# A table of gates laid out by expert, through a small scratch in DRAM, in an attention and two-layer mixture-of-experts kernel

## The chip, the cores and the metric

The kernel runs on one core of one Trainium2 chip. The metric is the device time of one execution in microseconds (us). Of the kernel before three executions were timed; their median is 2020.06 us.

## The reference

Attention over 4 batches, 8 heads, 576 positions and 64 values per head (local in heads 0 to 3, strided in heads 4 to 7) gives a matrix x of N = 2304 tokens by 512. The first layer mixes eight experts densely, with weights P from a Sinkhorn iteration. The second layer sends each token to exactly one expert, each expert with room for 288 tokens, in the order of the logits.

```python
def _moe_ref(x, w_gate, w1, w2):          # first layer: x (2304, 512), 8 experts, 1024 hidden
    logits = x @ w_gate
    P = np.exp(logits - logits.max())
    for _ in range(8):
        P /= P.sum(1, keepdims=True) + 1e-09
        P /= P.sum(0, keepdims=True) + 1e-09
        P *= N / E
    for e in range(E):
        out += P[:, e:e + 1] * (np.maximum(x @ w1[e], 0.0) @ w2[e])

def _moe2_ref(x, w_gate, w1, w2):         # second layer, on the output of the first
    logits = x @ w_gate                   # w_gate (512, 8)
    order = np.argsort(-logits.flatten())
    ...                                   # each token to the first expert in this order that has room
    for e in range(E):
        out[assigned == e] = np.maximum(x[assigned == e] @ w1[e], 0.0) @ w2[e]
```

## The kernel before

The work is one long program for five engines, written out in Python loops.

**Start.** Attention (`attention`, 0 to about 300 us) is cut into pieces. The string `SEQ` is the hand-written order in which its pieces (A), the preparation of the first expert's weights (W, V; R loads the second matrix), the first pieces of the next batch (E) and the first products of the first expert (Q) are issued. In this part every engine takes its instructions in the order in which they are written. That holds for the queue on which SyncE issues DMAs too (SPq in the profile); an issue that must wait holds up all issues behind it. Ahead of the loop over `SEQ` stand the load of the first expert's first matrix (L1443, 2 MB), that of the first layer's gates (L653) and that of the second layer's gates into the tile `wg2` (L1445). `wg2` (128 partitions x 4 x 8 floats) is not read by anything in the kernel before. The E pieces follow: `att_early` loads v of the next batch head by head (`att_load_v`, L176 to L179), waits `EPAD` = 3 pieces, and takes the largest absolute values on VectorE (`att_scale`, L207 and L210).

**First layer.** For each expert and each block of 512 tokens (256 for the first expert), `l1` makes 8 banks of 12 products (L729), and each bank is emptied by ScalarE into `hh` (L732) and by VectorE into `hl` (L733). There are three such banks, so TensorE waits when L733 is late. `l2` makes 24 products for a tile of 128 tokens (L747), and VectorE adds the result to `acc` (L779). `blocks` alternates the first product of one block with the second product of the block before. `weave` mixes other pieces in between in a fixed proportion, and `behind` queues each piece behind the last emptying of a bank.

**Logits of the second layer.** They are needed for routing, and are formed on VectorE in float32. `logits` (L904) multiplies a tile of `acc` (128 x 512) by the gates of one expert, which `gate_bcast` has copied into every partition, and sums along the row. Eight instructions make a tile's logits. The tiles named in `LATE` (8 to 15) get theirs woven into the last but one block order, before the last expert's share is added (1417 to 1506 us); for them `late_w` has multiplied the last expert's second matrix by the gates (L929, two halves of 256 columns, 128 instructions, 820 to 946 us), and `late_logits` adds that share by small products (L954, L955). The other ten tiles get their logits at once behind their last `l2` (1556 to 1694 us), next to `x2_rows` (L871 to L888), which scales and stores the tokens' rows.

`gate_bcast` loads rows d0 to d0 + n of the gates, 512 x 8 floats in memory, into each partition as they lie: the eight experts' gates of one row are next to each other, so the gates of one expert, `g[:, :, e]`, are read in steps of 8 floats.

**Second layer.** `routing` closes one expert after another, in pieces between the products that are left, and `ffn` computes the experts (to the end).

Of the kernel before, what the change touches and what calls it, by code (L numbers as in the profile page):

```python
# [33 lines left out]
# the order of the pieces of attention (A), both matrices of the first expert (W, V; R loads the second), what comes  # L34
# early of the second batch (E), products of the first expert (Q) and the gates (G, H)
# [29 lines left out]
class Arena:  # L65
    """Tiles as parts of others that are no longer needed."""
# [25 lines left out]
class Kernel:  # L92
# [11 lines left out]
    def abank(self, b, name):  # L104
        """While there is no first layer yet, attention has its banks too."""
        return self.bank(name, "l1" if b == 0 and name in ("ps", "po") else "bank")
# [5 lines left out]
    def pow2_scale(self, pool, top, mx, name):  # L112
        """From |max| in every partition: the power of two that takes it into [top/2, top), and its inverse."""
        nc = self.nc
        s = pool.tile([128, 1], F32, name=name)
        i = pool.tile([128, 1], F32, name=name + "_i")
        nc.vector.tensor_scalar(i, mx, 2.0 / top, 1e-30, op0=OP.mult, op1=OP.max)
        nc.vector.tensor_scalar(i.bitcast(I32), i.bitcast(I32), 0x7F800000, None, op0=OP.bitwise_and)
        nc.vector.reciprocal(s, i)  # L119
        return s, i  # L120

    # ---------------------------------------------------------------- attention
    def att_consts(self, pool):
# [3 lines left out]
        # local: query q and key window position k (key = q0 - 32 + k): 1 <= k - q <= 32  # L127
# [9 lines left out]
        # strided: position 4 i + r; the same r, and no later i  # L137
# [18 lines left out]
    def busy(self, ps, n):  # L156
        """Products that nothing needs, in front of those of a bank: the clock of the array follows its load."""
# [4 lines left out]
    def att_load_v(self, b, parts=None):  # L162
        """v of a batch: of every kind and head a part with room for a last column."""
# [35 lines left out]
    def att_scale(self, b):  # L199
        """The scale of a batch, from its values."""  # L200
# [17 lines left out]
        # token c * 128 + p belongs to batch token // 576  # L218
# [11 lines left out]
    def att_v(self, b, kind):  # L230
        """v in two halves, the high one with a column of ones, in 4 pieces."""
# [28 lines left out]
    def att_qk(self, u):  # L260
        """q and k of a pair of heads, transposed and in two halves."""
# [29 lines left out]
    def att_s(self, u, j):  # L291
        """Scores of one head, masked."""
# [27 lines left out]
    def att_e(self, u, j, i):  # L320
        """The exponentials of the scores of one head, first or second half."""
# [5 lines left out]
    def att_s_exact(self, u, j, kq, sm):  # L327
        """The same by products in float32, with the masks added and the sums taken on the way."""
# [56 lines left out]
    def over(self, x, ov, name):  # L385
        """Values over the sums of their weights."""
# [7 lines left out]
    def att_o(self, u, j):  # L394
        """The exponentials of one head, transposed."""
# [23 lines left out]
    def att_o2(self, u, j):  # L419
        """The values of one head, by the exponentials, over their sums."""  # L420
# [37 lines left out]
    def attention(self):  # L458
        """Attention, in pieces; after the last one of a batch its number is yielded."""
# [77 lines left out]
    def att_side(self, b):  # L537
        """What a batch does next to its heads: the second half of its v, and the first of that of the next one."""
# [10 lines left out]
    def att_early(self, pool):  # L549
        """What of the second batch comes before its heads, in 18 + EPAD pieces."""  # L550
# [10 lines left out]
    # ---------------------------------------------------------------- weights  # L561
# [8 lines left out]
    def loading(self):  # L570
        """Pieces without work, for as long as a matrix comes in."""
# [10 lines left out]
    def w_scale(self, r, j, inv, early):  # L582
        """The scale of a matrix of an expert; inv: the inverses of both of its matrices, multiplied."""
# [43 lines left out]
    def w_prep(self, e, w, raw=None, js=(0, 1)):  # L627
        """The weights of an expert of the first layer in two halves, in 8 pieces each."""
# [21 lines left out]
    # ---------------------------------------------------------------- gates of the first layer  # L650
# [19 lines left out]
    def gate(self, c0, c1):  # L670
        """Logits of tiles c0 to c1."""
# [15 lines left out]
    def sinkhorn(self):  # L687
# [7 lines left out]
        # the eighth power of the exponential of an eighth: the table is closest near 0  # L695
# [22 lines left out]
    # ---------------------------------------------------------------- the first layer  # L718
    def l1(self, w, t0, nb, h):
        """h = relu(x w1), transposed and in two halves."""  # L720
# [16 lines left out]
    def l2(self, w, t0, nb, h, done, fine=False):  # L737
        """y = h w2 of a tile of tokens, handed to done."""
# [44 lines left out]
    def pairs(self, jobs, pool, nb):  # L783
        """jobs as those of blocks: the first products of two, then the second ones, in small pieces."""
# [8 lines left out]
    def blocks(self, jobs, pool, nb, fine=False):  # L793
        """jobs: (expert, weights, first token, tokens); the first product of one runs before the second of the one before."""
# [11 lines left out]
    def weave(self, *gens):  # L806
        """(generator, its weight): all of them, evenly; a piece yields its weight, or weighs 1."""
# [9 lines left out]
    def behind(self, gen):  # L817
        """Every piece is queued behind what empties the last bank of a product traced before it."""
# [8 lines left out]
    def traced(self):  # L827
        """The last instructions so far of the engines that the pieces run on."""
# [15 lines left out]
    # ---------------------------------------------------------------- between the layers  # L844
    def m2_prep(self, e):
        """The weights of an expert of the second layer, in two halves, to DRAM, in 16 pieces."""
# [19 lines left out]
    def x2_rows(self, c):  # L866
        """A tile of tokens of the second layer, scaled by token and in two halves, to DRAM."""
# [32 lines left out]
    def logits(self, c):  # L900
        """Of a tile of tokens, of what is summed so far."""
        for e in range(E):
            junk = self.m2.tile([128, DM], F32, name="junk")
            self.nc.vector.scalar_tensor_tensor(junk, self.acc[:, c], 1.0, self.wgb[:, :, e], op0=OP.mult,  # L904
# [4 lines left out]
    def gate_bcast(self, o, d0, n):  # L909
        """The gates of the second layer in every partition, rows d0 on."""  # L910
        g = self.a["moe2_w_gate"]
        self.nc.sync.dma_start(out=o, in_=bass.AP(tensor=g.tensor, offset=g.offset + d0 * E, ap=[[0, 128], [1, n * E]]))
        return o.rearrange("p (d e) -> p d e", e=E)

    def late_w(self):
        """The second matrix of the last expert, times the gates of the second layer, in two halves, in 65 pieces."""
# [3 lines left out]
        for i in range(2):  # L920
# [5 lines left out]
            for c in range(FC):  # L926
                for e in range(E):
                    junk = self.m2.tile([128, DM], F32, name="junk")
                    nc.vector.scalar_tensor_tensor(junk[:, :n], w[:, c], 1.0, g[:, :, e], op0=OP.mult, op1=OP.mult,  # L929
# [14 lines left out]
    def late_logits(self, t0, nb, h):  # L944
        """What the last expert adds to the logits of a block, from its first product."""
# [17 lines left out]
    # ---------------------------------------------------------------- the second layer: who goes where  # L963
    def route_consts(self):
# [30 lines left out]
        # the state: who is free, room (far from any count once closed), closed experts, the assignment  # L995
# [8 lines left out]
        # rows that the first list takes another way  # L1004
# [7 lines left out]
    def search(self, key, oh, remc, base, first):  # L1012
        """The largest threshold, from base on, where an expert has as many keys as room."""
# [24 lines left out]
    def route(self, ph):  # L1038
        """Close one expert: every token that goes somewhere before it is full is assigned."""
# [13 lines left out]
        # the order of floats as that of two 16-bit numbers; 0 for tokens that have their place  # L1053
# [17 lines left out]
        # counts at the threshold and above it  # L1071
# [12 lines left out]
        # of every expert: the tokens above, and those at the threshold  # L1084
# [7 lines left out]
        # the first expert that is full, in ones, and its rows of weights  # L1092
# [471 lines left out]
```

## Time and profile before

| | |
|---|---|
| median of three runs | 2020.06 us (2018.05 to 2022.18) |
| profiled execution, first to last instruction | 2046.9 us |
| mean granted clock of TensorE in it | 0.974 |
| TensorE busy | 1944.9 us, 95% |
| VectorE busy | 1253.3 us, 61% |
| L904 on VectorE | 144 instructions, 156.2 us |
| L929 on VectorE | 128 instructions, 79.6 us |

The profiled execution is one execution, and no time but its span is known for it: the span is its own time here, 1.3% above the median of the runs. An engine is busy while one of its instructions runs; TensorE's matmuls overlap, so the mean of one is longer than the distance to the next. A wait names the instruction that waited and what released it. The granted clock is a share of full speed.

### The profile page before, as it was taken

What the parts mean: (1) busy time and instruction counts of PE and PEld (TensorE: products, weight loads), DVE (VectorE), ACT (ScalarE), POOL (GpSimd) and SP (SyncE); (2) the same over time, 40 slices, a digit from 0 to 9 for tenths busy, and PEclk for the clock granted to TensorE, in tenths of its full rate; (3) what the DMA queues carried; (4) which work ended last, traced back from release to release, by engine and by line L of the source; (5) the groups of instructions that cost most, each with busy time, mean ns of one, the idle gap of its engine ahead of it and who ended that gap; (6) DMA issues with size and microseconds to landing.
All of it is one profiled execution on the core that took longest, in us unless ns stands there. A gap on an engine that the chain in (4) does not pass through costs nothing.

```text
span 2046.9 us, 30815 instructions
## 1 busy us (share of the span) xinstructions
PE 1944.9 (95%) x12796; PEld 1102.4 (54%) x12796; DVE 1253.3 (61%) x2934; ACT 542.8 (27%) x1053; POOL 192.4 (9%) x272
## 2 busy tenths in 40 slices
PE   8899999999999999999999999999899889998997
PEld 7768676444544544454445444545354334676676
DVE  7777668365545545875555465435956898765530
ACT  5555553132222222111221222212101100122232
POOL 1433300000000000000000000000000002222231
PEclk9789999999999999999999999999999999999999
DMA  8212102024313431111243234401000002335350
GB/s 206 61 36 63 24 30 96 1 83 164 117 50 134 162 114 42 42 42 42 83 146 110 74 113 154 144 29 54 0 1 11 21 21 98 133 117 189 118 212 24
DMA packets 106300, 172.04 MB, mean 84 GB/s; under 512 B 61456, under 2 KB 64016, under 8 KB 101680
## 3 DMA queue, kind: packets, MB, share of 16 engines
q1 hardware_dynamic: 98480, 127.07, 18.8%
q0 software_dynamic: 7680, 43.01, 5.9%
q8 instruction: 100, 1.64, 0.3%
q14 instruction: 40, 0.33, 0.0%
HBM read 126.53 MB, written 43.53 MB: 83 GB/s over the span
## 4 chain that ended last, share of the span: by engine, by line
PE 60%; DVE 25%; DMA 7%; issue 4%; ACT 2%; POOL 1%; another core or an unknown queue 1%; SPq 0%; POOLq 0%; DVEq 0%; ACTq 0%
PE l L729 23%; PE l L747 23%; DVE junk L904 6%; DMA raw<-in_moe_w_dram 5%; PE mm L1384 3%; DVE junk L929 3%; DVE wmx L588 3%; PE mm L1356 2%; DVE hl L733 2%; DVE acc L779 1%; DVE m2l L616 1%; DVE w2l L616 1%; PE pcnt L1025 1%; DVE w1l L616 1%
## 5 line engine op out<-in xcount | busy, mean ns | idle before, releaser
L729 PE MATMUL l<-xh,w1h 128*128 128x512 f16 (+1 forms) x1408 | 484.5, 344 | 41.9 <-DVE hl L733 41.3
L729 PE MATMUL l<-xl,w1h 128*128 128x512 f16 (+1 forms) x1408 | 484.3, 344 | 0.0
L729 PE MATMUL l<-xh,w1l 128*128 128x512 f16 (+1 forms) x1408 | 484.1, 344 | 0.0
L747 PE MATMUL l<-w2h,hh 128*128 128x512 f16 x1152 | 438.1, 380 | 0.0
L747 PE MATMUL l<-w2l,hh 128*128 128x512 f16 x1152 | 437.8, 380 | 0.0
L747 PE MATMUL l<-w2h,hl 128*128 128x512 f16 x1152 | 437.5, 380 | 0.0
L729 PEld LDWEIGHTS <-w1h 128*128 128x128 f16 x2816 | 276.1, 99 | 276.5 <-issue 54.9
L732 ACT ACTIVATE hh<-l 128x512 f16<-128x512 f32 (+1 forms) x352 | 180.7, 517 | 805.9 <-PE l L729 805.7
L747 PEld LDWEIGHTS <-hh 128*128 128x128 f16 x2304 | 222.3, 98 | 258.7 <-issue 3.3
L733 DVE SCALAR_TENSOR_TENSOR hl<-l,hh 128x512 f16<-128x512 f32 (+1 forms) x352 | 205.6, 591 | 221.4 <-ACT hh L732 221.4
L779 DVE SCALAR_TENSOR_TENSOR acc<-l,pe,acc 128x512 f32<-128x512 f32 x126 | 94.2, 748 | 176.2 <-PE l L747 176.2
L729 PEld LDWEIGHTS <-w1l 128*128 128x128 f16 x1408 | 139.2, 99 | 114.4 <-issue 3.0
L747 PEld LDWEIGHTS <-hl 128*128 128x128 f16 x1152 | 113.0, 98 | 136.6 <-issue 1.3
L588 DVE TENSOR_REDUCE wmx<-raw 128x1 f32<-128x1024 f32 x120 | 141.2, 1210 | 65.6 <-DMA raw<-in_moe_w_dram 65.5
L904 DVE SCALAR_TENSOR_TENSOR junk<-acc,raw 128x512 f32<-128x512 f32 x144 | 156.2, 1084 | 3.3 <-DMA raw<-in_moe_w_gate_dram 1.4
L612 ACT ACTIVATE m2h<-raw,wscale 128x1024 f16<-128x1024 f32 x64 | 70.4, 1141 | 187.8 <-DVE iw L601 85.2
L616 DVE SCALAR_TENSOR_TENSOR m2l<-raw,wscale,m2h 128x1024 f16<-128x1024 f32 x64 | 80.1, 1281 | 45.6 <-DMA wd<-m2l 28.2
L594 POOL PARTITION_ALL_REDUCE wall<-wmx x32 | 11.3, 352 | 974.2 <-DVE wmx L592 974.2
L929 DVE SCALAR_TENSOR_TENSOR junk<-raw 128x256 f32<-128x256 f32 x128 | 79.6, 622 | 12.5 <-DMA raw<-in_moe_w_dram 9.0
L1361 DVE SCALAR_TENSOR_TENSOR h2l<-mm,h2h 128x288 f16<-128x288 f32 x64 | 28.8, 452 | 61.6 <-ACT h2h L1360 53.8
L612 ACT ACTIVATE w2h<-raw,wscale 128x1024 f16<-128x1024 f32 x28 | 30.1, 1137 | 94.9 <-DVE wscale L119 94.9
L1360 ACT ACTIVATE h2h<-mm 128x288 f16<-128x288 f32 x64 | 25.2, 411 | 91.8 <-PE mm L1356 66.5
(379 smaller groups left out, 2173.9 us busy)
## 6 DMA issues: line engine op xcount, KB each, us to landing
raw<-in_moe_w_dram SPq DMA_DIRECT2D x30, 2048.0 KB
wd<-m2h SPq DMA_DIRECT2D x32, 512.0 KB
wd<-m2l SPq DMA_DIRECT2D x32, 512.0 KB
q<-in_q_dram SPq DMA_DIRECT2D x32, 144.0 KB
k<-in_k_dram SPq DMA_DIRECT2D x32, 144.0 KB
acc<-in_moe_w_dram SPq DMA_DIRECT2D x2, 2048.0 KB
raw<-in_moe_w_gate_dram SPq DMA_DIRECT2D x2, 1024.0 KB
raw<-in_moe_w_dram SPq DMA_DIRECT2D x2, 1024.0 KB
```

The source lines that it names most:

```text
L588: nc.vector.tensor_reduce(mx[:, k:k + 1], r[:, k * n:k * n + n], axis=AX.XY, op=OP.max, apply_absolute_value=True)
L612: nc.scalar.activation(hi, raw, AF.Copy, scale=s1)
L616: nc.vector.scalar_tensor_tensor(lo, raw, s, hi, op0=OP.mult, op1=OP.subtract)
L729: nc.tensor.matmul(ps, l[:, d, fs], r[:, d, t0:t0 + nb], start=k == 0, stop=k == 3 * DC - 1)
L732: self.last = [nc.scalar.activation(hh[:, f, :nb], ps, AF.Relu).ins, nc.vector.scalar_tensor_tensor(hl[:, f, :nb], ps, 0.0, hh[:, f, :nb], ...
L733: nc.vector.scalar_tensor_tensor(hl[:, f, :nb], ps, 0.0, hh[:, f, :nb], op0=OP.max, op1=OP.subtract).ins]
L747: nc.tensor.matmul(ps, l[:, f, js], r[:, f], start=k == 0, stop=k == 3 * FC - 1)
L779: self.last = [nc.vector.scalar_tensor_tensor(a, ps, pe[:, c:c + 1], a, op0=OP.mult, op1=OP.add).ins]
L904: self.nc.vector.scalar_tensor_tensor(junk, self.acc[:, c], 1.0, self.wgb[:, :, e], op0=OP.mult, op1=OP.mult, accum_out=self.lg[:, c, e:e ...
L929: nc.vector.scalar_tensor_tensor(junk[:, :n], w[:, c], 1.0, g[:, :, e], op0=OP.mult, op1=OP.mult, accum_out=part[:, i, c, e:e + 1])
L1356: nc.tensor.matmul(ps, l[:, d, fs], xg[:, r], start=k == 0, stop=k == 3 * DC - 1)
L1384: nc.tensor.matmul(ps, l[:, f, dsl], r[:, f], start=k == 0, stop=k == 3 * FC - 1)
```

## The change

Three things change in the code; the rest of the diff takes out comments and docstrings and is left out here.

- A scratch of 8 x 512 floats is set up in DRAM (`gt`), and right after the load of `wg2` four stores write it there by expert, one for each 128 rows.
- `gate_bcast` copies from `gt` instead of the input, so that each partition holds the gates of expert 0, then those of expert 1, and so on.
- `logits` and `late_w` read `wgb[:, e]` and `g[:, e]`, 512 or 256 floats in a row.

```diff
     def logits(self, c):
...
-            self.nc.vector.scalar_tensor_tensor(junk, self.acc[:, c], 1.0, self.wgb[:, :, e], op0=OP.mult,
+            self.nc.vector.scalar_tensor_tensor(junk, self.acc[:, c], 1.0, self.wgb[:, e], op0=OP.mult,
                                                 op1=OP.mult, accum_out=self.lg[:, c, e:e + 1])
...
     def gate_bcast(self, o, d0, n):
-        g = self.a["moe2_w_gate"]
-        self.nc.sync.dma_start(out=o, in_=bass.AP(tensor=g.tensor, offset=g.offset + d0 * E, ap=[[0, 128], [1, n * E]]))
-        return o.rearrange("p (d e) -> p d e", e=E)
+        o = o.rearrange("p (e d) -> p e d", e=E)
+        self.nc.sync.dma_start(out=o, in_=self.gt[:, d0:d0 + n].unsqueeze(0).to_broadcast([128, E, n]))
+        return o
...
-                    nc.vector.scalar_tensor_tensor(junk[:, :n], w[:, c], 1.0, g[:, :, e], op0=OP.mult, op1=OP.mult,
+                    nc.vector.scalar_tensor_tensor(junk[:, :n], w[:, c], 1.0, g[:, e], op0=OP.mult, op1=OP.mult,
...
         self.xd = dram.tile([N, XR], F16, name="xd")
+        self.gt = dram.tile([E, DM], F32, name="gt")
...
                 nc.sync.dma_start(out=self.wg2, in_=self.a["moe2_w_gate"].rearrange("(c p) e -> p c e", p=128))
+                for c in range(DC):
+                    nc.sync.dma_start(out=self.gt.rearrange("e (c p) -> p c e", p=128)[:, c], in_=self.wg2[:, c])
                 for c in SEQ:
```

## Rows read from the trace of the kernel before

**Rows 1.** The page: busy time by engine; VectorE's busy tenths in 40 slices.

```profile
PE 1944.9 (95%) x12796; PEld 1102.4 (54%) x12796; DVE 1253.3 (61%) x2934; ACT 542.8 (27%) x1053; POOL 192.4 (9%) x272
...
DVE  7777668365545545875555465435956898765530
```

**Rows 2.** Waits of TensorE (total us, times, longest): whole span, then 1400 to 1760 us.

```profile
PE l L729 <- DVE hl L733: 41.3, 27, 7.4
...
PE l L729 <- DVE hl L733: 28.4, 11, 7.4
```

**Rows 3.** Busy time in three stretches: length, then each engine's busy us, clock, DMA.

```profile
820.00:946.00 126.00, 120.51 (x602) 58.72 (x601) 101.75 (x300) 13.60 (x28) 0.35 (x1) 1.00 0.11 36
1417.00:1506.00 89.00, 76.35 (x362) 35.81 (x361) 82.48 (x152) 10.28 (x19) 1.32 (x3) 0.96 0.06 24
1556.00:1694.00 138.00, 121.36 (x604) 54.26 (x601) 123.67 (x255) 14.33 (x24) 10.33 (x11) 0.95 0.05 20
```

**Rows 4.** The same right after the longest wait.

```profile
1460.00:1465.00 5.00, 4.83 (x14) 1.83 (x14) 4.90 (x10) 0.16 (x1) 0.22 (x1) 0.60 0.00 0
```

**Rows 5.** The chain that ended last: start us, length us, a store, 96 products.

```profile
468.52 2.62 DMA wd<-m2l
...
534.52 20.72 PE l L747 x96
```

**Rows 6.** Groups of TensorE, 1417 to 1506 us, then 1556 to 1694 us.

```profile
L729 PE MATMUL l<-xh,w1l 128*128 128x512 f16 x60 | 23.5, 392 | 0.0
L747 PE MATMUL l<-w2h,hh 128*128 128x512 f16 x48 | 18.2, 379 | 0.0
L729 PE MATMUL l<-xh,w1h 128*128 128x256 f16 x14 | 4.1, 290 | 4.6 <-DVE hl L733 4.6
...
L729 PE MATMUL l<-xh,w1h 128*128 128x512 f16 x96 | 38.3, 399 | 15.8 <-DVE hl L733 15.7
L747 PE MATMUL l<-w2l,hh 128*128 128x512 f16 x79 | 29.9, 379 | 0.0
L954 PE MATMUL pl<-lw,hh 128*128 128x16 f16 x40 | 2.2, 169 | 0.0
```

**Rows 7.** Groups of VectorE, whole span: busy us, mean ns, idle before.

```profile
L904 DVE SCALAR_TENSOR_TENSOR junk<-acc,raw 128x512 f32<-128x512 f32 x144 | 156.2, 1084 | 3.3 <-DMA raw<-in_moe_w_gate_dram 1.4
L733 DVE SCALAR_TENSOR_TENSOR hl<-l,hh 128x512 f16<-128x512 f32 x224 | 152.8, 688 | 166.0 <-ACT hh L732 166.0
L929 DVE SCALAR_TENSOR_TENSOR junk<-raw 128x256 f32<-128x256 f32 x128 | 79.6, 622 | 12.5 <-DMA raw<-in_moe_w_dram 9.0
L253 DVE SCALAR_TENSOR_TENSOR xl<-ptx,xh 128x288 f16<-128x288 f32 x12 | 16.4, 1444 | 8.0 <-ACT xh L252 8.0
L253 DVE SCALAR_TENSOR_TENSOR kq<-pt,kq 128x288 f16<-128x288 f32 x6 | 2.7, 446 | 0.0
L705 DVE TENSOR_TENSOR p<-p,rs 128x144 f32<-128x144 f32 x8 | 2.4, 303 | 0.1
```

**Rows 8.** The DMA-issuing queue (SPq) in order of time: start us, length us.

```profile
18.82 0.51 SPq L1445 DMA_DIRECT2D wg<-in_moe_w_gate_dram  x1
19.37 3.61 SPq L176 DMA_DIRECT2D hh<-in_v_dram  x1
25.77 1.74 SPq L195 DMA_DIRECT2D q<-in_q_dram  x2
...
31.29 0.39 SPq L176 DMA_DIRECT2D hl<-in_v_dram  x1
```

**Rows 9.** VectorE in order of time, with what ended its idle time.

```profile
27.65 2.35 DVE L588 TENSOR_REDUCE wmx<-acc 128x1 f32<-128x1024 f32 x2 [0.51 <-DMA acc<-in_moe_w_dram]
36.47 0.54 DVE L207 TENSOR_REDUCE vmx<-hl 128x1 f32<-128x384 f32 x1
```

**Rows 10.** DMA between 26 and 34 us; busy time between 36 and 48 us.

```profile
DMA packets 4252, 1.33 MB, mean 166 GB/s; under 512 B 4100, under 2 KB 4100, under 8 KB 4251
...
36.00:48.00 12.00, 8.72 (x97) 7.16 (x96) 11.06 (x37) 9.02 (x31) 0.35 (x1) 0.98 0.97 255
```

## The prediction

> **What bounds the kernel now.** I read the page first, then the waits of TensorE, then the busy time by stretch. TensorE is busy 95% of the span and VectorE 61%, so over the whole span TensorE sets the pace, but VectorE's slices reach 8 or 9 at the 17th (from 819 us) and from the 29th to the 34th (1433 to 1740 us) [rows 1]. The waits say what that costs: of the evictions by L733 that TensorE waited for, 28.4 of 41.3 us lie between 1400 and 1760 us [rows 2], where the logits of the second layer are formed. Three stretches hold the lines that the change speeds up [rows 3]: 820 to 946 us (L929, the late weights; VectorE busy 101.75 of 126), 1417 to 1506 us (L904 on the tiles named LATE, 82.48 of 89) and 1556 to 1694 us (L904 on the other tiles, 123.67 of 138). In each VectorE is the engine that is late: a bank of a first product isn't emptied in time because its L733 stands behind logits on VectorE's queue.
>
> What the stretches lose is more than idle time. Right after the longest wait (7.4 us) the granted clock is 0.60 over 5 us, so TensorE ran at the lower of its two levels there [rows 4]. So I count the products instead. 96 products of 512 columns take 20.72 us at full clock, 0.216 each [rows 5]; one of 256 columns is taken as half. From 1417 to 1506 us there are three kinds x60 and three x48 of 512 and three x14 of 256 (where records are missing I take the fuller kind): 324 x 0.216 + 42 x 0.108 = 74.4 us of work in 89, 14.6 lost [rows 6]. From 1556 to 1694 us: 3 x 96 + 3 x 79 = 525 x 0.216 = 113.3, and two kinds of small products of 2.2 us, together 117.7 in 138, 20.3 lost. From 820 to 946 us the clock is 1.00 and 126 - 120.5 = 5.5 us are idle [rows 3]. So 40.4 us is the most that a faster VectorE can give back.
>
> **Part 1, the products read contiguous floats.** Now L904 takes 1084 ns for 512 floats and L929 622 ns for 256, 1.80 ns for each float more [rows 7]. What they cost with contiguous operands no row shows exactly. Nearest is the same instruction in L733, 512 elements in runs, one operand in PSUM: 688 ns. Two SBUF float operands, p contiguous and one repeated over it, take 303 ns for 144 (L705). The slope between them is (688 - 303) / 368 = 1.05 ns, which gives 303 + 112 x 1.05 = 420 ns for 256. I take 688 and 420, since both the slope and the type fit. The bounds: no change at all, and 688 or 420 (no row has a float pair faster than that). So a logit saves 0.396 us and a late weight 0.202: 144 x 0.396 = 57.0 and 128 x 0.202 = 25.9 us of VectorE. The accumulator reads stay.
>
> That a step is what costs is shown elsewhere in the profile: L253 on 128x288 takes 446 ns where it writes in runs (kq) and 1444 ns where two operands go in steps of 8 elements (xl, xh of the strided heads) [rows 7].
>
> What of the 82.9 us reaches TensorE? Late weights: VectorE's 101.75 falls to 76 in 126; I take back 4.5 of 5.5 us, since the stretch starts with VectorE waiting for its load. LATE tiles: 82.48 - 63 x 0.396 = 57.5 against 74.4 of products; I take 14 of 14.6. The other tiles: 123.67 - 80 x 0.396 = 92.0 against 117.7; but logits come in bunches of 8 per tile behind the second products, so some backlog stays: I take 17 of 20.3. Together 35.5 us, with bounds 27 (half of the last stretch kept) and 40.4. The rest of the 82.9 is time in which TensorE is busy anyway.
>
> **Part 2, the scratch.** New are four stores on the DMA-issuing queue, right behind the load of the gates (L1445). A store reads what that load writes, so the queue stands at the first one until the load has landed. Before, it went straight on: the load was issued at 18.82 and the next batch's v at 19.37 us [rows 8]. The load is issued behind the 2 MB of L1443, and these released VectorE at 27.65 us [rows 9]; so the queue is held from 19.4 to about 27.7. While it is held the DMA engines run dry, since they worked off what had been issued by then.
>
> Then the stores themselves. Each goes from 128 partitions x 8 floats to places 2 KB apart, so 4-byte runs: 4 x 1024 = 4096 packets. Between 26 and 34 us 4252 small packets went in 8 us, 531 per us [rows 10]: 4096 / 531 = 7.7 us. I take that pace, as packets of 256 B and less made it; below it only the four issues at 0.51 us, 2 us. Above it, no row shows 4-byte writes to DRAM. If the four stores wait for one another, it is four turns instead of one; a store to DRAM stands in the chain with 2.62 us [rows 5], so that adds some 10.
>
> Behind the stores stand the v loads of the next batch (L176 to L179) and the q and k of the fourth pair of heads (L195, 25.77) [rows 8]. So loads that ran from about 26 us on (an estimate: behind the 2 MB, whose landing VectorE saw at 27.65) now start at about 27.7 + 1 + 7.7 = 36.4, 10 us later. Who waits: VectorE at L207 (36.47 us) reads v of the third head, whose load was issued at 31.29 [rows 8], and didn't wait for it [rows 9]. Its slack is at most 5.2 us (36.47 - 31.29). By their shapes 4928 packets stood ahead of it (two heads of v, 1312 each, and 2304 of q and k) and 640 are its own: 5568 / 531 = 10.5 us from 26 us on is 36.5, so it came just in time; I take a slack of 1. VectorE then stands 9 us with the whole attention behind it. It can't make that up soon: from 36 to 48 us it is busy 11.06 of 12 us [rows 10]. TensorE, 8.72 of 12 there, has work that hangs on VectorE's. So I put the early loss at 9 us, between 2 (cheap stores, full slack) and 18 (the stores in turn).
>
> By the Trainium skill (DMA: Bandwidth & Descriptors, Specifications and Rules for kernel authors) a last dimension that isn't contiguous becomes one descriptor per element, and under 512 B a write is read, modified and written. It speaks against this change. If it doubles a packet's price, the stores take 15.4 us and the early loss is 17 instead of 9, total 2001.5; no run so far shows it.
>
> **Part 3, the loads from the scratch.** They come 800 us after the stores, so they wait for nothing new. The whole table is read in runs as before. The two half tables become eight runs of 1 KB per partition, 1024 packets each, 2 us at the pace above. In that stretch TensorE loses 5.5 of 126 us, so its products cover it: 0, and at most 2 us each if they don't. The code of removed comments costs nothing.
>
> **Sum.** -35.5 + 9 = -26.5 us. The profiled execution's span is 2046.9, 26.8 above the median of the runs, 2020.06; I carry the difference over in us: **1993.5 us**.
>
> **The rivals.**
>
> - The step isn't the price (the instruction has two SBUF float operands and an accumulator, and no row has all three in runs): L904 stays near 1084 ns, nothing comes back, and the early loss stands: 2020 + 9 = 2029, slower. For it: L733's second operand is in PSUM. Against: L705 reads two SBUF operands at 1.05 ns a float, and 1.80 isn't that. It decides where the gain is under 9 us, about a quarter of the saving, so above some 980 ns for L904. Chance 0.08.
> - The held queue costs more: stores in turn, or dearer packets, 15 to 30 us early: 2000 to 2015. Only over 35 us does it end slower. For it: VectorE has no room from 36 to 48 us [rows 10]. Against: 531 packets per us is what small packets made there. Over 35 us would need 4096 packets at under 130 per us. Chance 0.15, and 0.03 beyond 35 us, about 2030. The rule of the Trainium skill (DMA: Bandwidth & Descriptors, Rules for kernel authors) cited above points this way.
> - The early loss is hidden, by slack in the loads or because attention makes it up later: 2 us instead of 9, 2020 - 35.5 + 2 = 1986.5, down to 1981 with all 40.4. Chance 0.12.
> - VectorE gets faster but TensorE still waits, because VectorE's queue keeps its order and hl stands behind bunches of logits: half the gain, -18 + 9 = 2011. Against: 117.7 - 92.0 = 25.7 us of room in the last stretch. Chance 0.07.
>
> The forecast itself, 1984 to 2005, has 0.55.
>
> **How the numbers follow.** 0.2% is 4 us, about what a measurement of this kernel can tell from no change. Faster: 0.55 + 0.12 + 0.13 of the held queue + 0.05 of the bunches = 0.85; slower: 0.08 + 0.03 + 0.01 = 0.12; the same 0.03. The range 1979 to 2012 holds the forecast, the hidden loss and most of the held queue.
>
> **What would show it.** Right: L904 near 690 and L929 near 420 ns; TensorE's wait for L733 from 1400 to 1760 us down from 28.4 to under 8; the clock at 1.00 in the two late stretches; an SPq wait of some 8 us in front of the first store, and VectorE waiting for a load of v near 36 us for 5 to 10 us. Wrong: L904 over 900 ns; the first store going out without a wait; an early stage longer by over 20 us; or waits for L733 that stay although L904 is short.

## The result, and the profile after

The changed kernel takes 1996.5 us (median of four runs, 1987.1 to 2001.7) against 2019.5: 0.988 of before, 95% interval 0.986 to 0.991. The prediction was 1993.5 in a range of 1979 to 2012, so direction and time hold. Of the sum, -35.5 + 9, both terms turn out too small, and most of the error of one is hidden by that of the other: that the time came out so close is luck in part.

**Where the time came from.** The groups of VectorE of the kernel after, whole span, answer to [rows 7]:

```profile
L904 DVE SCALAR_TENSOR_TENSOR junk<-acc,raw 128x512 f32<-128x512 f32 x144 | 98.9, 687 | 3.3 <-DMA raw<-gt 1.4
L929 DVE SCALAR_TENSOR_TENSOR junk<-raw 128x256 f32<-128x256 f32 x128 | 54.1, 423 | 11.6 <-DMA raw<-in_moe_w_dram 8.1
```

687 and 423 ns stand where the prediction had 688 and 420. The table from the scratch keeps L904 waiting 1.4 us in all, so reading it costs nothing. The waits of TensorE, whole span, answer to [rows 2]; the columns are total us, times and the longest:

```profile
PE pt L282 <- DMA k<-in_k_dram: 26.4, 3, 24.9
...
PE l L729 <- DVE hl L733: 6.6, 9, 2.0
```

The wait for L733 fell from 41.3 to 6.6 us. At the top of the list is a new one: TensorE waits 24.9 us at a stretch for a load of k. The three stretches of [rows 3] in the kernel after, between the same matmuls (both traces have 12,796 in one order):

```profile
846.60:967.20 120.60, 119.83 (x603) 58.82 (x602) 78.51 (x302) 14.36 (x28) 0.35 (x1) 1.00 0.16 47
1438.20:1511.60 73.40, 73.40 (x361) 35.19 (x360) 59.43 (x156) 9.92 (x19) 1.32 (x3) 1.00 0.07 29
1560.50:1675.40 114.90, 114.90 (x605) 53.19 (x604) 92.72 (x257) 14.33 (x24) 6.25 (x11) 1.00 0.06 24
```

They are 5.4, 15.6 and 23.1 us shorter (126, 89 and 138 before), and 1.1 comes from the 50 us between the last two: 45.2 us. In both late stretches TensorE is busy throughout at a clock of 1.00.

**Where it went.** The DMA-issuing queue of the kernel after, in order of time (start us, length us), answers to [rows 8]:

```profile
18.56 0.64 SPq L1446 DMA_DIRECT2D wg<-in_moe_w_gate_dram  x1
19.31 6.03 SPq L1010 DMA_DIRECT2D xd<-z  x4
28.06 2.25 SPq L1448 DMA_DIRECT2D gt<-wg  x4
30.36 6.93 SPq L176 DMA_DIRECT2D hh<-in_v_dram  x1
37.34 3.71 SPq L178 DMA_DIRECT2D hh<-in_v_dram  x1
41.09 2.22 SPq L179 DMA_DIRECT2D hh<-in_v_dram  x1
43.40 3.18 SPq L195 DMA_DIRECT2D q<-in_q_dram  x2
46.63 7.78 SPq L195 DMA_DIRECT2D k<-in_k_dram  x2
54.46 1.35 SPq L176 DMA_DIRECT2D hh<-in_v_dram  x1
```

The four stores go out at 28.06, where the prediction had 27.7. Four stores of zeros (L1010), issued at 55.08 before, now stand ahead of them. They are written behind the loop over `SEQ`, so the order of this queue is not wholly the written one. The four stores are issued in 2.25 us, so none waits for the one before it. But then the loads behind them take 2 to 8 us to issue, and the next head's v goes out at 54.5 instead of 29.7. VectorE in order of time, at its first wait for these loads, answers to [rows 9]:

```profile
55.24 0.55 DVE L207 TENSOR_REDUCE vmx<-hh 128x1 f32<-128x384 f32 x1 [20.06 <-DMA hh<-in_v_dram]
```

And TensorE at its own:

```profile
58.55 0.95 PE L282 MATMUL pt<-identf,k 72*128 72x72 f32 x6 [24.89 <-DMA k<-in_k_dram]
```

The DMA engines of the kernel after between 28 and 54 us answer to [rows 10]; the second line is GB/s in 40 slices:

```profile
DMA  0379693477699999309999999569999956759654
GB/s 15 3 6 5 1 1 0 1 1 0 1 1 1 0 0 0 0 0 1 0 5 14 4 33 34 10 20 49 80 44 19 38 19 50 40 50 95 65 99 109
DMA packets 5944, 0.59 MB, mean 23 GB/s; under 512 B 5862, under 2 KB 5872, under 8 KB 5944
```

The engines are busy and move next to nothing: at most 1 GB/s from 30.6 to 41 us. 5944 packets in 26 us are 229 per us, where the prediction took 531.

**A note on the span.** The changed kernel's profiled execution took 2001.7 us (span 1999.7). The profile of before has a span of 2046.9, and 29 us of the difference lie in the second layer. The experiments ran on three chips: on two of them the kernel before takes 2046 to 2047 us, on the third 2017.5. From the matmul at 1763 us on to the end, the kernel before takes 283.5 us in its first profile and 282.3 in the second (first run below); the changed kernel takes 254.3 here and 285.4 on the chip of `e8_after`. So the long second layer goes with the chip and not with the change, and the 26.8 us that the prediction carried over as one execution's own are the chip's. Every ratio is taken against the kernel before on the same chip, and the stages before 1765 us can be compared across chips.

### The profile page after: what moved, and what is told of

Same layout as the page of the kernel before. It is cut to its first block, busy times and chain, and to the rows that moved or that the text cites. A ratio compares the mean times of both kernels' runs of the same rounds, so it can differ in the third digit from the quotient of the medians.

```text
span 1999.7 us, 30821 instructions
## 1 busy us (share of the span) xinstructions
PE 1930.3 (97%) x12796; PEld 1103.2 (55%) x12796; DVE 1173.5 (59%) x2934; ACT 544.0 (27%) x1053; POOL 188.8 (9%) x272
## 5 line engine op out<-in xcount | busy, mean ns | idle before, releaser
L733 DVE SCALAR_TENSOR_TENSOR hl<-l,hh 128x512 f16<-128x512 f32 (+1 forms) x352 | 206.3, 590 | 233.4 <-ACT hh L732 233.2
L904 DVE SCALAR_TENSOR_TENSOR junk<-acc,raw 128x512 f32<-128x512 f32 x144 | 98.9, 687 | 3.3 <-DMA raw<-gt 1.4
L929 DVE SCALAR_TENSOR_TENSOR junk<-raw 128x256 f32<-128x256 f32 x128 | 54.1, 423 | 11.6 <-DMA raw<-in_moe_w_dram 8.1
L325 ACT ACTIVATE sm<-sm,mx 72x72 f32<-72x72 f32 (+1 forms) x168 | 49.0, 369 | 1.5 <-DVE mx L317 1.4
```

The source lines that it names most:

```text
L325: self.nc.scalar.activation(sm[:, g], sm[:, g], AF.Exp, bias=mx[:, g:g + 1], scale=1.0 / math.sqrt(D))
L733: nc.vector.scalar_tensor_tensor(hl[:, f, :nb], ps, 0.0, hh[:, f, :nb], op0=OP.max, op1=OP.subtract).ins]
```

## The experiments

For each run the start of the same matmul is compared with that in the second profile of before (`e0_before`). The table is worked out from the traces: its first line has that matmul's start in `e0_before`, the others how many us later it starts (minus: earlier).

| at this matmul of before | 38 | 126 | 858 | 940 | 1429 | 1567 | 1711 | ratio to before, 95% |
|---|---|---|---|---|---|---|---|---|
| the changed kernel | 26.2 | 28.0 | 29.8 | 24.1 | 23.9 | 5.9 | -18.4 | 0.988 (0.986 to 0.991) |
| the same, another chip (`e8_after`) | 24.0 | 16.9 | 16.8 | 11.2 | 10.7 | -7.2 | -33.2 | 0.991 (0.989 to 0.993) |
| stores only (`e2_stores_only`) | 25.2 | 27.2 | 28.1 | 28.1 | 27.1 | 25.7 | 24.8 | 1.011 (1.010 to 1.013) |
| runs of 32 bytes (`e3_runs32`) | 8.7 | -1.2 | -1.5 | -1.5 | -1.5 | -3.0 | -3.9 | 1.004 (1.003 to 1.006) |
| no wait (`e7_no_hold`) | 18.2 | 11.5 | 10.9 | 11.0 | 10.7 | 9.6 | 8.7 | 1.008 (1.006 to 1.011) |
| 64 bytes apart (`e4_spread`) | 10.6 | 12.6 | 13.8 | 13.9 | 13.4 | 13.2 | 13.1 | 1.002 (1.001 to 1.004) |
| only the rows apart (`e9_rows_apart`) | 50.4 | 50.4 | 50.8 | 50.6 | 49.9 | 48.8 | 47.9 | 1.025 (1.022 to 1.029) |
| stores late (`e1_late`) | -1.1 | -1.0 | 0.2 | -5.5 | -6.5 | -24.4 | -50.4 | 0.978 (0.976 to 0.979) |
| the same again (`e11_late_again`) | -2.1 | -2.0 | -1.9 | -7.6 | -7.3 | -25.3 | -51.2 | 0.976 (0.974 to 0.979) |
| stores late, late weights in steps (`e6_late_w_steps`) | -1.7 | -2.7 | -2.0 | -2.2 | -2.4 | -20.3 | -44.6 | 0.978 (0.977 to 0.980) |
| stores late, logits in steps (`e10_logits_steps`) | -1.3 | 1.3 | 1.5 | -4.1 | -4.5 | -5.0 | -5.1 | 0.996 (0.994 to 0.997) |

**The kernel before once more.** No edit.

> The kernel before, unchanged, profiled once more. If the 29 us by which the changed kernel's second layer (from 1763 us on) was shorter belong to the one profiled execution of before, the span here is about 2018 to 2022 us and the second layer takes as long as in the changed kernel, to within 5 us. If they belong to the change, the span is again near 2047 us.

2047.35 us, span 2045.3: again the long second layer, and 17 other runs of this kernel on the same chip have a median of 2046.1. Its matmuls lie within 4 us of those of the first profile from start to end. The span is near 2047 us again, but not for the reason that was written beside it: `e8_after` has the long second layer with the change in it. So the 29 us belong to the chip, not to one execution and not to the change. What the first profile names there are waits of ScalarE for something off the core ("remote", 21.9 us in the second layer of before). Every profile with the long second layer lists such waits, and none with the short one does; what they are stays open.

**The four stores alone.** In the kernel before:

```diff
+        self.gt = dram.tile([E, DM], F32, name="gt")
...
+                for c in range(DC):
+                    nc.sync.dma_start(out=self.gt.rearrange("e (c p) -> p c e", p=128)[:, c], in_=self.wg2[:, c])
```

> The kernel before, with the four stores of the gates to a scratch at the place where the changed kernel has them; nothing reads the scratch. Theory A: slower by the whole early loss, 24 to 30 us, about 2046 us. By the prediction's size of the loss, 9 us: 2028 us. If the queue that waits and the other stores that move ahead are all of it, the same 24 to 30 us here, and in the next run too.

2069.06 against 2046.1, 23 us slower. TensorE stands 22.4 us for k and is 25 to 28 us late from there to the end. The early loss is of the stores, and nothing later gives it back.

**The same wait with 32-byte runs.** The scratch in the input's order, 512 packets:

```diff
+        self.gt = dram.tile([DM, E], F32, name="gt")
...
+                    nc.sync.dma_start(out=self.gt.rearrange("(c p) e -> p c e", p=128)[:, c], in_=self.wg2[:, c])
```

> The kernel before, with four stores of the same gates at the same place and behind the same wait, but in the order of the input: runs of 32 bytes, 512 packets in place of 4096; nothing reads them. Theory A (the packets): slower by 8 us or less, 2021 to 2028 us. Theory B (the queue that stands still until the gates have landed, and the stores of zeros that move ahead of the loads): slower by 24 to 30 us, as with the four-byte stores.

2055.72 against 2046.1; the ratio, 1.0044, is 9.0 us (5 to 13): near theory A's bound, far from B's. TensorE stands 7.7 us for k. The runs spread from 2043 to 2064 us, and the profiled one is the fastest; the clock, below, is the likeliest reason (its mean is 0.981 in the fastest run and 0.966 in the slowest). So the held queue, with the zeros that moved ahead and 512 packets, is a loss of its own, of some 9 us here; a run below with the same wait measures 4.

**The same packets without the wait.** As the stores alone, but the source is a tile of ones:

```diff
-                    nc.sync.dma_start(out=self.gt.rearrange("e (c p) -> p c e", p=128)[:, c], in_=self.wg2[:, c])
+                    nc.sync.dma_start(out=self.gt.rearrange("e (c p) -> p c e", p=128)[:, c], in_=self.onesf[:, 8 * c:8 * c + 8])
```

> The kernel before, with four stores of 4096 four-byte packets at the same place, but from a tile of ones that is there from the start, so that the queue does not wait for the gates and the stores of zeros stay where they were; nothing reads the scratch. The stores alone cost 1.0114 of before with the wait, four stores in 32-byte runs 1.0044. If packets and wait add up, the packets alone are worth the difference: about 1.007, 14 us. If the wait only matters because the packets come behind it with empty engines (packets beside the 2 MB load are hidden): 1.000 to 1.003. If the packets are all of it: 1.011.

2063.0 against 2047.36, 1.0084 (1.006 to 1.011), nearest to the first case. TensorE stands 13.5 us for k. The two prices add up: 0.44% for the held queue and 0.84% for the packets are 1.28%, and both together measured 1.14% (0.97 to 1.32). But the run doesn't separate them cleanly. Its queue is not free either, because the stores themselves take 14 us to issue:

```profile
19.98 13.96 SPq L1448 DMA_DIRECT2D gt<-onesf  x4
33.98 2.25 SPq L176 DMA_DIRECT2D hh<-in_v_dram  x1
```

The next batch's v goes out at 33.98, no sooner than in `e3_runs32` (32.76).

**The packets 64 bytes apart.** The same wait, the same 4096 packets of 4 bytes, other addresses:

```diff
+        self.gt = dram.tile([E, DM * 16], F32, name="gt")
...
+                    nc.sync.dma_start(out=self.gt.rearrange("e (c p s) -> p c e s", p=128, s=16)[:, c, :, 0], in_=self.wg2[:, c])
```

> As the kernel of before with the four early stores that nothing reads, the same wait and the same 4096 four-byte packets, but each 64 bytes from the next in DRAM, where they had been side by side. If the price is the packet (a fixed time for each): 1.011 of before, and the packets last as long in the trace, some 20 us. If it is many engines writing into the same 64 bytes: as with 32-byte runs, 1.004, and the packets are gone in 8 us.

2053.07 against 2047.36, 1.002 (1.001 to 1.004), 4.3 us and the second case. TensorE stands 8.8 us for k, 1.1 more than with 512 packets (the table's 13 us later on are of the profiled execution, the slowest of twelve). The DMA engines of this run between 28 and 48 us:

```profile
DMA  2010004777991699985427899999999998999999
GB/s 59 30 18 0 18 5 4 7 7 6 6 3 11 75 96 74 125 124 116 114 50 167 199 216 185 185 215 160 232 231 155 202 263 156 186 216 264 250 348 348
DMA packets 10307, 2.56 MB, mean 128 GB/s; under 512 B 9705, under 2 KB 9751, under 8 KB 10306
```

The low stretch (slices 7 to 12) lasts 3 us, and the loads run from 34.5 us on. The same window with the packets side by side, stores alone:

```profile
DMA  6953699548999999999999999499923764026997
GB/s 17 40 2 1 3 2 1 1 0 0 1 1 0 1 1 1 0 0 0 0 1 0 1 1 0 1 0 0 0 0 0 0 1 5 4 26 59 107 57 28
DMA packets 4733, 0.18 MB, mean 9 GB/s; under 512 B 4724, under 2 KB 4732, under 8 KB 4732
```

Here the low stretch lasts from 29 to some 45 us. So it isn't the packet, its 4 bytes or their number.

**Only the rows apart.** The large scratch of the run before, but side by side within a row:

```diff
-                    nc.sync.dma_start(out=self.gt.rearrange("e (c p s) -> p c e s", p=128, s=16)[:, c, :, 0], in_=self.wg2[:, c])
+                    nc.sync.dma_start(out=self.gt[:, 0:DM].rearrange("e (c p) -> p c e", p=128)[:, c], in_=self.wg2[:, c])
```

> As the run with the packets 64 bytes apart, with the same scratch, whose eight rows lie 32 KB apart, but within a row the four-byte packets lie side by side again. If neighbours in the same 64 bytes are the price: as the changed kernel's own stores, 1.011 of before, the packets last some 20 us in the trace and TensorE stands some 25 us. If it was that the whole scratch lay in one 16 KB: as with 64 bytes apart, 1.002, TensorE stands some 10 us.

2067.68 against 2017.53 on this chip: 50 us slower. The neighbours are the price, not the small scratch. It is even dearer than expected. TensorE's longest waits for k, the last figure of each line, in the runs with stores only, runs of 32 bytes, no wait, 64 bytes apart and only the rows apart:

```profile
PE pt L282 <- DMA k<-in_k_dram: 23.0, 2, 22.4
PE pt L282 <- DMA k<-in_k_dram: 7.7, 1, 7.7
PE pt L282 <- DMA k<-in_k_dram: 14.9, 3, 13.5
PE pt L282 <- DMA k<-in_k_dram: 10.1, 3, 8.8
PE pt L282 <- DMA k<-in_k_dram: 49.8, 1, 49.8
```

That this chip doubles the price is unlikely: on it the same stores in rows 2 KB apart, issued late, take no longer than on another chip (`e11_late_again` below, 15.0 us against 15.4). That leaves the rows 32 KB apart, which one run shows and none explains.

**The stores late.** In the changed kernel they move to the end of the first gate's normalization, where DMA is idle; an added zero makes them wait for it:

```diff
+        z1 = self.cons.tile([128, 1], F32, name="z1")
+        nc.vector.tensor_scalar(z1, self.pe0[:, 0:1], 0.0, None, op0=OP.mult)
+        wg3 = self.cons.tile([128, DC, E], F32, name="wg3")
+        nc.vector.tensor_scalar(wg3, self.wg2, z1, None, op0=OP.add)
+        for c in range(DC):
+            nc.sync.dma_start(out=self.gt.rearrange("e (c p) -> p c e", p=128)[:, c], in_=wg3[:, c])
```

> The changed kernel with its four stores to the scratch moved from the start to about 376 us, behind the end of the first gate's normalization (a dependency through an added zero), where no transfer is urgent. Theory A (the 4096 four-byte packets hold up the loads of v, q and k, 28 us): the early loss is gone, about 1969 us, at most 1977. Theory B (the early loss is small, as the prediction had it, 9 us, and the rest of the 28 us is of one execution): about 1985 to 1988 us. If the stores late cost as much as they do early: 1997 us, as the changed kernel.

2002.33 against 2046.1, 0.9775 (0.976 to 0.979). On the chip of the first measurement that would be 0.9775 x 2019.5 = 1974 us, within theory A's 1969 to 1977. The early loss is gone: TensorE is 1 us ahead of before at 126 us, and the whole late gain stays. The DMA engines of this run between 370 and 410 us, 40 slices of 1 us, show the stores by themselves:

```profile
DMA  0000069999999999999130000000000000000000
GB/s 0 0 16 0 0 5 4 1 1 1 1 1 0 0 0 0 0 0 0 1 1 0 0 0 0 0 0 0 0 0 16 0 0 0 0 0 0 0 0 0
DMA packets 4162, 0.05 MB, mean 1 GB/s; under 512 B 4160, under 2 KB 4160, under 8 KB 4160
```

With nothing beside them they still take some 15 us (375 to 391), and up to 389 us they keep the 16 engines busy. The loads of v, q and k had only to stand behind that.

**The changed kernel on another chip.** No edit.

> The changed kernel, unchanged, on the same chip as the other experiments: 0.988 of before, as measured, so some 1.1% over the same with its stores moved to 376 us. If the chips differ in more than the length of the second layer, another ratio.

2030.67 against 2047.36, 0.991 (0.989 to 0.993), with runs from 2015.6 to 2032.0; the stores moved late are 1.3% better. The profiled run is the fastest (mean clock 0.980; 0.969 to 0.972 in the four runs over 2030 us), and it shows where such spreads are likely to come from. The granted clock is the number behind the engines' columns. First the profiled execution of the changed kernel, then that of this run:

```profile
48.00:58.00 10.00, 0.00 (x0) 0.00 (x0) 0.62 (x2) 0.00 (x0) 0.35 (x1) 0.50 0.70 94
58.00:68.00 10.00, 9.45 (x59) 8.03 (x60) 3.08 (x10) 1.47 (x3) 0.00 (x0) 0.50 0.97 284
68.00:78.00 10.00, 10.00 (x65) 8.39 (x66) 6.76 (x22) 4.59 (x14) 0.00 (x0) 0.50 0.66 126
```

```profile
48.00:58.00 10.00, 1.17 (x8) 1.14 (x9) 0.85 (x3) 0.12 (x1) 0.35 (x1) 0.50 0.75 135
58.00:68.00 10.00, 9.82 (x98) 8.70 (x98) 5.78 (x21) 4.69 (x16) 0.00 (x0) 0.85 1.01 282
68.00:78.00 10.00, 8.97 (x102) 7.54 (x101) 9.51 (x32) 7.00 (x20) 0.58 (x3) 1.00 0.70 150
```

In both TensorE stands some 25 us and its clock falls to half (1.2 GHz). In the first it is still at half from 58 to 78 us, when the engine works again (124 matmuls), and stays there to 108 us; in the second it is back (200). In the table the first ends the start 28 us late and the second 17, having been 26 and 24 late at 38 us.

The other runs show the same. Here are the same 694 products, those between the matmuls of 38 and 126 us, in `e0_before`, `e3_runs32` and `e4_spread`:

```profile
37.50:125.50 88.00, 75.11 (x697) 64.66 (x696) 67.47 (x178) 51.39 (x139) 33.26 (x37) 0.77 0.34 82
46.30:124.40 78.10, 63.49 (x697) 55.00 (x696) 66.48 (x174) 49.64 (x134) 33.36 (x36) 0.91 0.34 77
48.10:138.10 90.00, 82.28 (x696) 70.72 (x696) 66.24 (x174) 49.44 (x134) 33.09 (x36) 0.69 0.29 66
```

They take 88 us at a mean clock of 0.77, 78 at 0.91 and 90 at 0.69. The kernel before runs part of this stretch at half clock itself, so a run whose clock is back sooner makes up its whole stall of 8 us, and another makes up nothing. The times of these variants are medians over both courses, and prices that are 5 us apart are not told apart by them.

**Late weights in steps again.** As the stores late, but `late_w` reads the gates from the input:

```diff
-            g = self.gate_bcast(r[:, 0:n * E], i * n, n)
+            gs = self.a["moe2_w_gate"]
+            self.nc.sync.dma_start(out=r[:, 0:n * E], in_=bass.AP(tensor=gs.tensor, offset=gs.offset + i * n * E,
+                                                                  ap=[[0, 128], [1, n * E]]))
+            g = r[:, 0:n * E].rearrange("p (d e) -> p d e", e=E)
...
-                    nc.vector.scalar_tensor_tensor(junk[:, :n], w[:, c], 1.0, g[:, e], op0=OP.mult, op1=OP.mult,
+                    nc.vector.scalar_tensor_tensor(junk[:, :n], w[:, c], 1.0, g[:, :, e], op0=OP.mult, op1=OP.mult,
```

> The changed kernel with the stores moved to 376 us, but the weights of the late logits read the gates from the input again, in steps of eight floats; the logits proper read contiguous floats. By the two traces the late weights gave TensorE 5.5 us: slower than with both by that, 0.9775 + 0.0027 = 0.980 of before. If the 26 us that VectorE saves there are hidden: 0.9775. If the queue of VectorE stays behind from there on: more than 0.985.

2001.74 against 2047.36, 0.978 (0.977 to 0.980). In the trace the first case is there: between 858 and 940 us this run gains 0.2 us where `e1_late` gains 5.7, and at 1711 it is 5.8 behind. The time doesn't show it: the interval is 3 us each way, and in the profiled executions this one makes 5 us up at the start of the second layer, where from 1700 to 1740 us its clock stays at 1.00 and that of `e1_late` falls to 0.83 and 0.91. So this run alone doesn't settle it; the next one does.

**Logits in steps again.** As the stores late, but `logits` reads the input's order, from a table loaded as it lies:

```diff
-            self.nc.vector.scalar_tensor_tensor(junk, self.acc[:, c], 1.0, self.wgb[:, e], op0=OP.mult,
+            self.nc.vector.scalar_tensor_tensor(junk, self.acc[:, c], 1.0, self.wgb[:, :, e], op0=OP.mult,
```

> The changed kernel with the stores moved to 376 us and the late weights on contiguous floats, but the logits proper read the input's order, in steps of eight floats. If the two parts of the gain are as the traces place them (late weights 5.5 us, logits some 40): TensorE 5.5 us ahead of before from 950 us to the end of the first layer, and 0.997 of before. If the late weights' part is given back later: 1.000. If the logits alone were not worth more than the prediction's 31 us: 0.9775 + 0.0151 = 0.993.

2008.39 against 2017.53, 0.996 (0.994 to 0.997). TensorE gains 5.6 us between 858 and 940 us and keeps them (-4.1 at 940, -5.1 at 1711). The late weights' part is there and isn't given back; 0.0043 x 2017.5 = 8.7 us (5 to 12) is somewhat more.

**Both, on this chip.** No edit to the stores late.

> The changed kernel with the stores moved to 376 us, once more, beside the two parts of the gain: 0.9775 of before again, within 0.002. By the sum of the parts (0.978 with the logits' part alone, and what the other run gives for the late weights' part): 0.975 to 0.978.

1968.31 us against 2017.53, 0.976 (0.974 to 0.979), 49 us faster than before and the shortest time of all. The DMA engines between 370 and 410 us, 40 slices of 1 us, show the stores on this chip, from 373.6 to 388.6 us:

```profile
DMA  0002999999999999952000000000000000000000
```

**The step of the second operand.** In the kernel before each expert's logits read 512 floats of the table at another step:

```diff
-            self.nc.vector.scalar_tensor_tensor(junk, self.acc[:, c], 1.0, self.wgb[:, :, e], op0=OP.mult,
-                                                op1=OP.mult, accum_out=self.lg[:, c, e:e + 1])
+            stt = self.nc.vector.scalar_tensor_tensor
+            x, lg = self.acc[:, c], self.lg[:, c, e:e + 1]
+            g = self.wgb.rearrange("p d e -> p (d e)")[:, 0:(e + 1) * DM].rearrange("p (d s) -> p d s", s=e + 1)[:, :, 0]
+            if e == 0:
+                stt(junk, x, 1.0, g, op0=OP.mult, op1=OP.mult, accum_out=lg)  # 1
...
+            else:
+                stt(junk, x, 1.0, g, op0=OP.mult, op1=OP.mult, accum_out=lg)  # 8
```

> The kernel before, whose logits read, as the second operand, the first 512 floats of the table in steps of 1 for the first expert, 2 for the second, up to 8 for the last, each on a line of its own; the logits are not those of the reference, and only the times of these lines are read. If any step costs: 687 ns at step 1 and some 1084 from step 2 on. If a step costs by the bytes that it passes over: a rise with the step, up to 1084 at step 8. If it costs from some size on: two levels with the jump between, at 16 bytes or at 32.

The groups of VectorE; L908 has step 1, L910 step 2, and so on to L922 with 8:

```profile
L922 DVE SCALAR_TENSOR_TENSOR junk<-acc,raw 128x512 f32<-128x512 f32 x18 | 19.6, 1087 | 0.3
...
L914 DVE SCALAR_TENSOR_TENSOR junk<-acc,raw 128x512 f32<-128x512 f32 x18 | 19.5, 1081 | 0.3
...
L912 DVE SCALAR_TENSOR_TENSOR junk<-acc,raw 128x512 f32<-128x512 f32 x18 | 15.3, 850 | 0.3
L910 DVE SCALAR_TENSOR_TENSOR junk<-acc,raw 128x512 f32<-128x512 f32 x18 | 12.4, 689 | 0.2
L908 DVE SCALAR_TENSOR_TENSOR junk<-acc,raw 128x512 f32<-128x512 f32 x18 | 12.4, 686 | 1.6 <-DMA raw<-in_moe_w_gate_dram 1.5
```

Step 2 is free, step 3 costs 41% of the full price, (850 - 686) / (1084 - 686), and from 4 to 8 it is flat (1075 to 1087). So the third case: the full price is reached at 16 bytes. That what counts is how many floats share 16 bytes fits, step 3 included, where two of four floats have such a neighbour. The Trainium skill (SBUF — State Buffer, Specifications (TRN2)) says that SBUF has lines of 16 bytes and needs two hits per line for full speed; this trace agrees, with 689 ns at two floats per line and 1081 at one.

## Why the prediction was right, and where its terms were off

- **Part 1, the products.** Right to 3 ns, and the rival that the step isn't the price falls. Steps of 2 would have done as well.
- **What reaches TensorE.** 35.5 predicted, 45.2 measured, above the bound of 40.4. Late weights 5.4 for 4.5. LATE tiles 15.6 for 14: the products need 73.4 us, not 74.4. Other tiles 23.1 for 17: the backlog that was to stay is not there (no wait for L733 is left among those listed from 1420 us on), and the products need 114.9 us, not 117.7. That need was counted too high, and so the bound was too low. Where kinds of product differed in number the prediction took the fuller one, as if records were missing, but the stretch's edge had cut a group: 321 and 40 are there, not 324 and 42. And it added the small products by their busy time, 4.4 us, which overlaps that of the others: 524 products of 0.216 us leave under 2 of the 114.9 us for all 81 of them. By the table, against the second profile of before, the kernels with both parts gain 48 to 51 us between 858 and 1711 us; with the late weights in steps 42.6 are left, so the logits' part is 43 and the late weights' 5 to 6.
- **Part 2, the held queue.** Right: until 28.06 us, though the zeros fill 6 us of the wait. With 512 packets it costs 9.0 us by time, with 4096 quick ones 4.3, and TensorE stands 7.7 and 8.8 us (`e3_runs32`, `e4_spread`). That is up to the size the whole early loss was to have.
- **Part 2, the stores.** This is the step that failed: "I take that pace", 531 packets per us. That row's small packets were loads, nearly all of 256 B. 4096 stores of 4 bytes side by side take some 15 us by themselves (some 270 per us); the loads behind them issue slowly, and VectorE waits 20 us and TensorE 25, not 9. An early stage longer by over 20 us was among the signs that the prediction named for being wrong, and it is there. What moves the loss further is the clock after the stall. The upper bound of 18 rested on stores in turn, and they don't take turns. The second rival, dearer packets, is what happened: 28 us early in the profiled execution, 17 in the other profile, 23 as a time by itself. Beside a wait of 20 us the slack of 1 us for L207 hardly matters.
- **The page cited there.** The Trainium skill (DMA: Bandwidth & Descriptors, Specifications) has writes under 512 B read, modified and written; by it the early loss was to be 17 us. It points the right way, and the loss was larger still. But `e3_runs32` and `e4_spread` also write less than 512 B, 512 times 32 and 4096 times 4, and there TensorE stands 7.7 and 8.8 us. So size or number alone isn't the price here.
- **Part 3.** Right: 0.
- **The sum.** -45.2 + 28 = -17 us in the profiled execution, -22.9 by the medians, where -26.5 was predicted. The two errors, 10 us too little gain and 14 to 19 too little loss, hide each other. Had only the early loss been known, the forecast would have been some 2010, and wrong by more: the direction was foreseen, the closeness of the time was luck.
- **What stays open.** Why neighbours are dear (that writes by several engines into the same few bytes of DRAM stand in one another's way fits, and no run looks inside), why rows 32 KB apart double it, and what decides when the clock comes back after a stall.

## What to carry to other kernels

Cost a store by what lies next to each packet in DRAM, and take a pace only from packets of the same size and direction; a transposing store of 4-byte elements side by side is best put where no transfer is wanted for 20 us, here 350 us later and well ahead of its reader. A store that must wait for a load holds every load behind it on the same queue, so look for what is queued there before placing it. To see what a stage can give back, compare its length with the plain products of an undisturbed stage, not with the busy time of the disturbed one.

## What the runs showed of the hardware

- 4096 stores of 4 bytes side by side in DRAM: some 15 us alone, a stall of 22 to 25 us for the loads behind; 64 bytes apart: gone in 3 us, a stall of 8.8, of which 7.7 come with 512 packets too.
- The second operand of a float product on VectorE, by step: 686, 689, 850, then 1075 to 1087 ns from step 4 on.
- After stalls of 23 and 25 us the clock of TensorE was back within 10 us in one execution and still at half some 50 us later in the other; with that the loss at 126 us was 17 and 28 us.
- The second layer of the same program took some 29 us longer on two chips than on a third (282 to 287 us against 254 to 256).
